# Backward weight products with 32x32 block transposes on VectorE in place of 128x128 transposes on TensorE

## The chip, the cores and the metric

The kernel runs on one core of a Trainium2 chip. A core has five engines with a queue each: TensorE (PE: matrix products and transposes into PSUM; its weight loads are shown as PEld), VectorE (DVE), ScalarE (ACT), GpSimd (POOL) and SyncE (SP, which here only issues loads). Sixteen DMA engines move data between HBM and the core's SBUF. The metric is the device time of one execution in microseconds. Lower is better.

## What is computed

A forward pass of four residual blocks for one new token of two sequences, and its whole backward pass. Blocks 1 and 3 are grouped-query attention over a long cache (32 query heads, 4 key/value heads, 16,384 positions, head size 128), blocks 2 and 4 an MLP (1024 to 3584 to 1024); both attention blocks share their weights, and so do both MLPs.

```python
def _A_ref(x, k_cache, v_cache, wq, wo):
    q = (x @ wq).reshape(B, Sq, Hq, Dh).transpose(0, 2, 1, 3)
    k, v = repeat(k_cache, rep), repeat(v_cache, rep)
    scores = einsum("bhqd,bhkd->bhqk", q, k) * (Dh ** -0.5)
    o = einsum("bhqk,bhkd->bhqd", softmax(scores), v)
    return o.transpose(0, 2, 1, 3).reshape(B, Sq, Hq * Dh) @ wo

def _B_ref(x, w1, b1, w2, b2):
    h = gelu(einsum("bsd,df->bsf", layernorm(x), w1) + b1)
    return einsum("bsf,fd->bsd", h, w2) + b2

x = A_x
x = x + _A_ref(layernorm(x), K, V, wq, wo)
x = x + _B_ref(layernorm(x), w1, b1, w2, b2)
x = x + _A_ref(layernorm(x), K, V, wq, wo)
x = x + _B_ref(layernorm(x), w1, b1, w2, b2)
out, grads = x, vjp(grad_out)   # gradients of x, K, V, wq, wo, w1, b1, w2, b2
```

In the backward pass every weight W [n_in, n_out] meets a gradient g of two columns: `W g`, a product over the columns of W. In memory W has its rows first, and a matrix product on PE sums over partitions. So W must be turned in some way before it can be multiplied. This case is about that turning.

## The kernel before

Everything is written out by hand in order (`manual_schedule`); each engine runs its queue in the order of the program, and a buffer's next load waits until the last reader of the buffer is done. Loads go into a pool `ld` of seven 1 MB buffers (`NLD = 7`, `LDW = 4096` columns of bf16 on 128 partitions). SP issues them in program order, so it runs ahead of the engines by up to seven buffers.

The stages in order, with their place in the profiled execution: attention forward of layer 0 (to about 172 us), passes over wo, w1 and w2 (to 257), q pass and attention forward of layer 1 (to 420), wo, w1 (to 448), then backward: w1 (453 to 474), wo (479 to 501), attention backward of layer 1 (502 to 660), then w2 (to 687), w1 (to 711) and wo (to 731) for layer 0, and the tail (from 732): attention backward of layer 0 with all outer products and the stores of the gradients.

*Weights as stationary operand.* A forward product needs no turning: `lhsT` is the weight block itself. `w_pass` (L288) does the forward product (L306), the backward product, or both on one load of W (w2 at L918, called w2a: forward of layer 0 and the product that layer 1's backward pass will need).

*Backward products.* `BwdPipe` (L260) takes a row of up to 1024 weights per partition: eight PE transposes into a PSUM bank (L270, tile `wtp`), one eviction to SBUF by ACT or DVE, whichever has been charged less (`evac_bf16`, L151; `charge`, `pick`), and two rows later eight products with the turned block as stationary operand and the gradient, repeated 16 times to 32 columns, as moving operand (L281).

*Ahead.* For the passes over w2 and wo of layer 0 (`w2b`, `wob`) the class `Ahead` (L343) turns rows in place before their gradient is there (`turn`, L318), so that PE and ACT turn rows while the layer norms in front run; `some(rest, n)` and the hooks of `ln_bwd` (L224) say how many. `copies_on("A")` (L139) sends those evictions to ACT. Products follow at L381. Every fifth row is not turned at all: `Dots` (L325) spreads the gradient along the free axis (L335), and DVE multiplies and sums the row, once per sequence (L339).

*wq in attention backward.* `attn_bwd` (L593) works in slots, one for each quarter of a V chunk. wq's four column quarters come in as their gradient gets ready (`wq_steps`, L877): the first two quarters and half of the third by dots (`by_dots`, L615), the rest by PE turns (L322, tile `wtq`) and products (L895).

*The tail.* Loads of K, V and wq come from a list of jobs (`load_next`, L1197; `pump`), evictions go to ACT or DVE by load, stores on POOL's queue. A quarter of wq is turned row by row (`late_pe`), and multiplied when its gradient is there. The last quarter's products (`in_rows`, L1281) are in front of the last layer norm.

*Loads of w1.* `w_chunks` (L245) gives one row block of 128 rows with all 3584 columns per load: 7,168 bytes in a row per partition. w2 and wo come as four row blocks of 1024 columns, 2,048 bytes in a row.

```python
tp = (pt if self.n % 3 else px)([128, 8, 128], BF16, "wtp")
for o in range(on):
    PE.transpose(tp[:, o, :], wv[:, j, (o0 + o) * 128:(o0 + o + 1) * 128], ident[:])
wT = ktp.tile([128, 8, 128], BF16, name="wT", tag="kT")
evac_bf16(wT[...], tp[...], on * 128)
...
PE.matmul(wide_out(self.out_ps, 2 * jj), lhsT=wT[:, o, :], rhs=wide_in(self.gT[:, o0 + o, :]), ...)
```

Of the kernel before, what the change touches and what calls it, by code (L numbers as in the profile page):

```python
# [23 lines left out]
def kernel(  # L24
# [24 lines left out]
    nc = tc.nc  # L49
# [72 lines left out]
    sel2v = sel2[:].rearrange("p (h t) -> p t h", t=2)  # L122
    e_all = pers.tile([128, G, NP, 2, 8, 2], BF16, name="e_all")
# [6 lines left out]
    V.memset(ACCT[:], 0.0)  # L130

# [128 lines left out]
    class BwdPipe:  # L260


        def __init__(self, out_ps, gT_bf, n_o):
            self.out_ps, self.gT, self.n_o, self.q, self.n = out_ps, gT_bf, n_o, deque(), 0

        def push(self, wv, j, jj, o0, on):
            self.n += 1
            tp = (pt if self.n % 3 else px)([128, 8, 128], BF16, "wtp")
            for o in range(on):
                PE.transpose(tp[:, o, :], wv[:, j, (o0 + o) * 128:(o0 + o + 1) * 128], ident[:])  # L270
            wT = ktp.tile([128, 8, 128], BF16, name="wT", tag="kT")
            evac_bf16(wT[:, 0:on, :].rearrange("p a b -> p (a b)"), tp[:, 0:on, :].rearrange("p a b -> p (a b)"),
                      on * 128)
            self.q.append((wT, jj, o0, on))
            if len(self.q) > 2:
                self.pop()

        def pop(self):
            wT, jj, o0, on = self.q.popleft()
            for o in range(on):  # L280
                PE.matmul(wide_out(self.out_ps, 2 * jj), lhsT=wT[:, o, :], rhs=wide_in(self.gT[:, o0 + o, :]),  # L281
                          start=(o0 + o == 0), stop=(o0 + o == self.n_o - 1))

        def flush(self):
            while self.q:
                self.pop()

    def w_pass(W, n_in, n_out, name, xT_bf=None, gT_bf=None, mid=None):  # L288

        JO, JI = n_out // 128, n_in // 128  # L290
        fps = bps = pipe = None
        if xT_bf is not None:
            nw = min(WIDE, 512 // JO)
            fps = ACCT[:, 0:JO * nw].rearrange("p (j b) -> p j b", b=nw)
            V.memset(fps, 0.0)
        if gT_bf is not None:
            bps = px([128, 512], F32, name + "_b")
            pipe = BwdPipe(bps, gT_bf, JO)
        for j0, rb in w_chunks(n_in, n_out):
            wv = w_load(W, j0, rb, n_out)  # L300
            if mid is not None and j0 == 4:
                mid()
            if fps is not None:
                for j in range(rb):
                    for jo in range(JO):
                        PE.matmul(fps[:, jo, :].rearrange("p (a b) -> p a b", b=2),  # L306
                                  lhsT=wv[:, j, jo * 128:(jo + 1) * 128],
                                  rhs=xT_bf[:, j0 + j, :].unsqueeze(1).to_broadcast([128, nw // 2, 2]),
                                  start=False, stop=True, skip_group_check=True)
            if bps is not None:  # L310
                for j in range(rb):
                    for o0 in range(0, JO, 8):
                        pipe.push(wv, j, j0 + j, o0, min(8, JO - o0))
        if pipe is not None:
            pipe.flush()
        return fps[:, :, 0:2] if fps is not None else None, pairs(bps, JI) if bps is not None else None
# [8 lines left out]
    class Dots:  # L325


        def __init__(self, name):
            self.rows = [ktp.tile([128, 2 * NB, 128], BF16, name=name, tag="blk", bufs=2) for _ in range(2)]
            self.junk = wrk.tile([128, D], BF16, name="junk", tag="rowout")  # L330

        def spread(self, b, col):
            tp = pt([128, 8, 128], BF16, "dotr")
            for o in range(8):
                PE.transpose(tp[:, o, :], col(o).to_broadcast([128, 128]), ident[:])  # L335
            evac_bf16(self.rows[b][:].rearrange("p a b -> p (a b)"), tp[:].rearrange("p a b -> p (a b)"), 1024)

        def dot(self, w, b, out):
            V.scalar_tensor_tensor(out=self.junk[:], in0=w, scalar=1.0, in1=self.rows[b][:].rearrange("p o d -> p (o d)"),  # L339
                                   op0=ALU.mult, op1=ALU.mult, accum_out=out)  # L340
            charge("D", 1.15)

    class Ahead:  # L343


        def __init__(self, W, n_in, name, xT_bf=None, fps=None):
            self.W, self.J, self.x, self.fps, self.name = W, n_in // 128, xT_bf, fps, name
            self.dotted = range(4, FJ, 5)
            self.dp = vec.tile([128, len(self.dotted), 2], F32, name=name + "_dp")
            self.chunks = list(w_chunks(n_in, D))  # L350
            self.rows = {}

        def load(self, k):
            j0, rb = self.chunks[k]
            wv = w_load(self.W, j0, rb, D)
            for j in range(rb):
                self.rows[j0 + j] = wv[:, j, :]

        def row(self, j):
            w = self.rows[j]  # L360
            if self.fps is not None:
                for jo in range(DJ):
                    PE.matmul(wide_out(self.fps, jo * WIDE), lhsT=w[:, jo * 128:(jo + 1) * 128],
                              rhs=wide_in(self.x[:, j, :]), start=False, stop=True, skip_group_check=True)
            if j not in self.dotted:
                turn(w, lambda: pt([128, 8, 128], BF16, "turn"))

        def spread(self, gT_bf):
            self.dd = Dots(self.name + "_g")
            for b in range(2):  # L370
                self.dd.spread(b, lambda o: gT_bf[:, o, b:b + 1])

        def dots(self, j):
            for b in range(2):
                self.dd.dot(self.rows[j], b, self.dp[:, self.dotted.index(j), b:b + 1])

        def products(self, j, out_ps, gT_bf):
            if j in self.dotted:
                return
            for o in range(8):  # L380
                PE.matmul(wide_out(out_ps, 2 * j), lhsT=self.rows[j][:, o * 128:(o + 1) * 128],  # L381
                          rhs=wide_in(gT_bf[:, o, :]), start=(o == 0), stop=(o == 7))
# [42 lines left out]
    class Acc:  # L425
# [3 lines left out]
        def __init__(self, g, src, coef, finish, half=0):  # L429
# [3 lines left out]
            self.acc = ACCT[:, half * 256:half * 256 + 256] if half < 2 else pm_([128, 256], F32, "acc2")[:]  # L433
# [158 lines left out]

    def attn_bwd(l, do_bf, dqT, dn, groups, ahead):  # L593
        sch = Sched()
        wq_q, wq_n, w2_q = deque(), {}, deque()
        slots = []
        for i, g in enumerate(groups):
            for c in range(NCH):
# [16 lines left out]
        def by_dots(kv):  # L615
# [7 lines left out]
            def item(j, b):  # L623
                if j % 4 == 0 and b == 0:
                    n[0][j // 4]()
# [918 lines left out]
```

## Time and profile before

| what | value |
|---|---|
| runs | 1138.20, 1139.32, 1139.52 us; median 1139.32 |
| span of the profiled execution | 1136.1 us |
| busy: PE | 945.3 us, 83% |
| busy: DVE | 637.6 us, 56% |
| busy: ACT | 567.5 us, 50% |
| mean granted TensorE clock | 0.882 |
| bytes moved | 449.24 MB, mean 395 GB/s |
| packets of the load queue q1 and the store queue q0, share of 16 engines | 77.4% and 19.7% |
| transposes of weights by `BwdPipe` (L270) | 928, 75.9 us |
| in-place turns of weights `wt` (L322) | 400, 31.1 us |
| dots of wq, w2, wo on DVE (L339) | 40, 10, 10; 48.8, 12.2, 12.3 us |
| in the chain that ended last | PE 50%, DMA 31%, DVE 10%, issue 4%, ACT 3% |

How to read it. The span is one execution under the profiler; the runs are timed without it. A busy share is an average over stages that have different limits: PE is busy 83% of the span, yet for most of it the DMA engines are what is full. The views by slice and by stage tell which it is where. In a line of groups, "x" is the number of instructions, then busy time and the mean duration of one; durations of instructions that follow each other overlap, so the time from start to start is shorter than the mean duration. Shares of DMA above 1 come from packets that overlap in the records. GB/s is the safer figure, but packets of 2 KB move at a lower rate than those of 8 KB even where the engines never stand.

### The profile page before, as it was taken

Reading aid. Unit: us, or ns where it says so; the run is one execution under the profiler, and the core shown is the slowest. Engines: PE = TensorE matmul, PEld = TensorE weight load, DVE = VectorE, ACT = ScalarE, POOL = GpSimd, SP = SyncE. Lnnn points to the kernel's source line nnn. Section 1 sums busy time; section 2 is a strip of 40 time slices with the busy share of each in tenths; the row PEclk is TensorE's granted clock in tenths of the full one; section 3 lists DMA queues with packets and bytes.
Section 4 is the critical chain, followed back from the end, with each engine's and each line's share of the span. In section 5 each row is a group of like instructions: output and inputs, shape, how many; then the busy total and the mean of one; then the engine's idle time right before and its main releaser. Section 6 shows DMA issues by size and latency. Waiting matters only on the chain.

```text
span 1136.1 us, 38923 instructions
## 1 busy us (share of the span) xinstructions
PE 945.3 (83%) x17087; PEld 715.0 (63%) x17087; DVE 637.6 (56%) x1391; ACT 567.5 (50%) x1414; POOL 70.1 (6%) x124
## 2 busy tenths in 40 slices
PE   4978796487879885899998699988898897898896
PEld 3867675487767665898876588855555454455452
DVE  1545442133545432444746454778788767787776
ACT  0544342022535340344554344767787756686674
POOL 0000000000000000000000000022111111111210
PEclk9988976596998976899998899999999978898987
DMA  9999999998999989999999999998999999999997
GB/s 371 424 424 424 424 425 412 405 379 354 423 426 424 423 320 422 392 350 393 380 422 418 359 371 336 364 367 311 394 418 423 423 419 423 424 412 421 422 402 288
DMA packets 91962, 449.24 MB, mean 395 GB/s; under 512 B 7302, under 2 KB 7302, under 8 KB 54672
## 3 DMA queue, kind: packets, MB, share of 16 engines
q1 hardware_dynamic: 74448, 354.46, 77.4%
q0 software_dynamic: 17344, 92.29, 19.7%
q8 instruction: 133, 2.18, 0.7%
q14 instruction: 37, 0.30, 0.1%
HBM read 348.14 MB, written 98.58 MB: 393 GB/s over the span
## 4 chain that ended last, share of the span: by engine, by line
PE 50%; DMA 31%; DVE 10%; issue 4%; ACT 3%; POOL 0%; DVEq 0%; POOLq 0%; ACTq 0%; SPq 0%
DMA kv_V<-in_A_v_cache_dram 13%; PE tp L420 10%; PE wtp L270 5%; DMA kv_K<-in_A_k_cache_dram 5%; PE tpm L1451 4%; PE acc_all L452 4%; PE xm L1260 4%; DMA wt<-in_A_wo_dram 3%; DMA out_dram<-keepK 3%; DMA keepK<-in_A_v_cache_dram 3%; PE sc L573 3%; PE turn L322 3%; PE xm L1174 3%; PE dp L1313 2%; DMA out_dram<-keepxV 2%
## 5 line engine op out<-in xcount | busy, mean ns | idle before, releaser
L153 ACT COPY kT<-tp 128x512 int32<-128x512 int32 x209 | 122.8, 587 | 256.7 <-PE tp L420 247.9
L156 DVE COPY kT<-tp 128x1024 bf16<-128x1024 bf16 x159 | 108.8, 691 | 110.0 <-PE tp L420 99.1
L420 PE MATMUL tp<-ident,kv_K 128*128 128x128 bf16 x1728 | 140.3, 228 | 4.5 <-DMA kv_K<-in_A_k_cache_dram 4.5
L420 PEld LDWEIGHTS <-kv_K 128*128 128x128 bf16 x1728 | 106.3, 102 | 5.4 <-DMA kv_K<-in_A_k_cache_dram 5.3
L164 DVE CAST big<-xm 128x512 bf16<-128x512 f32 x133 | 86.4, 685 | 16.2 <-PE xm L1260 11.2
L161 ACT CAST big<-xm 128x512 bf16<-128x512 f32 x151 | 82.2, 595 | 23.2 <-PE xm L1260 13.0
L573 PEld LDWEIGHTS <-kT 128*128 128x128 bf16 x2048 | 75.9, 98 | 27.3 <-issue 21.0
L573 PE MATMUL sc<-qT_bf,kT 128*128 128x8 bf16 x2048 | 91.7, 171 | 0.3 <-issue 0.3
L161 ACT CAST keepV<-xm 128x512 bf16<-128x512 f32 (+1 forms) x137 | 75.1, 594 | 28.5 <-PE xm L1260 16.6
L420 PE MATMUL tp<-ident,kv_V 128*128 128x128 bf16 x864 | 71.5, 231 | 11.5 <-DMA kv_V<-in_A_v_cache_dram 10.6
L270 PE MATMUL wtp<-ident,wt 128*128 128x128 bf16 x928 | 75.9, 229 | 4.3 <-issue 2.9
L537 ACT ACTIVATE e_all<-sc,negm 128x64 bf16<-128x64 f32 x256 | 77.2, 345 | 1.1 <-DVE negm L532 1.0
L164 DVE CAST keepV<-xm 128x512 bf16<-128x512 f32 (+1 forms) x101 | 66.1, 685 | 18.6 <-PE xm L1260 12.3
L306 PEld LDWEIGHTS <-wt 128*128 128x128 bf16 x1696 | 48.8, 103 | 42.9 <-issue 15.2
L452 PE MATMUL acc_all<-kv_V,e_all 128*16 128x256 bf16 x864 | 46.2, 294 | 29.7 <-DMA kv_V<-in_A_v_cache_dram 16.7
L156 DVE COPY wT<-wtp 128x1024 bf16<-128x1024 bf16 (+1 forms) x64 | 41.1, 645 | 47.7 <-PE wtp L270 43.9
L153 ACT COPY wT<-wtp 128x512 int32<-128x512 int32 (+1 forms) x60 | 34.1, 568 | 64.2 <-PE wtp L270 55.8
L420 PEld LDWEIGHTS <-kv_V 128*128 128x128 bf16 x864 | 56.7, 103 | 13.3 <-DMA kv_V<-in_A_v_cache_dram 11.3
L270 PEld LDWEIGHTS <-wt 128*128 128x128 bf16 x928 | 58.1, 102 | 5.0 <-issue 3.7
L537 ACT ACTIVATION_READ_ACCUMULATOR e_all<-sc,negm 128x1 f32 x256 | 60.1, 235 | 0.0
L161 ACT CAST keepK<-xm 128x512 bf16<-128x512 f32 x98 | 52.9, 596 | 13.5 <-PE xm L1260 7.6
L1313 PE MATMUL dp<-wdo,kT 128*128 128x64 bf16 x896 | 52.2, 205 | 0.0
(369 smaller groups left out, 1750.5 us busy)
## 6 DMA issues: line engine op xcount, KB each, us to landing
kv_K<-in_A_k_cache_dram SPq DMA_DIRECT2D x81, 1024.0 KB, 11.5
kv_V<-in_A_v_cache_dram SPq DMA_DIRECT2D x81, 1024.0 KB, 12.5
wt<-in_A_wo_dram SPq DMA_DIRECT2D x32, 1024.0 KB, 9.9
wt<-in_B_w_dram SPq DMA_DIRECT2D x32, 896.0 KB, 14.0
out_dram<-big POOLq DMA_DIRECT2D x26, 1024.0 KB, 19.0
out_dram<-keepV POOLq DMA_DIRECT2D x19, 1024.0 KB, 20.0
out_dram<-keepK POOLq DMA_DIRECT2D x17, 1024.0 KB, 17.8
wt<-in_A_wq_dram SPq DMA_DIRECT2D x16, 1024.0 KB, 9.0
```

Source lines behind the costliest of these rows:

```text
L153: S.copy(out=dst.bitcast(I32), in_=src.bitcast(I32))
L156: V.tensor_copy(out=dst, in_=src)
L161: S.copy(out=dst, in_=src)
L164: V.tensor_copy(out=dst, in_=src)
L270: PE.transpose(tp[:, o, :], wv[:, j, (o0 + o) * 128:(o0 + o + 1) * 128], ident[:])
L306: PE.matmul(fps[:, jo, :].rearrange("p (a b) -> p a b", b=2), lhsT=wv[:, j, jo * 128:(jo + 1) * 128], rhs=xT_bf[:, j0 + j, :].unsqueeze(1) ...
L420: PE.transpose(tp[:, j, :], cv[:, b * 8 + j, :], ident[:])
L452: PE.matmul(self.acc[cg:cg + 16, :], lhsT=coef(u), rhs=self.cv[:, t:t + 2, :].rearrange("p t d -> p (t d)"), start=False, stop=True, tile_ ...
L537: S.activation(out=e_all[:, g, f * half:(f + 1) * half, l, h, :], in_=sc[g][f][:, h, :].rearrange("p (a b) -> p a b", b=2), func=ACT.Exp, ...
L573: PE.matmul(sc[g][f][:, :, t % TH], lhsT=kT[:, j, :], rhs=q_bf[:, g, :], start=True, stop=True)
L1260: PE.matmul(pss[k][:], lhsT=blk[p:p + 64, o + 2 * h + k // 2, :], rhs=Qm[p:p + 64, :, :].rearrange("p a b -> p (a b)"), start=True, stop=T ...
L1313: PE.matmul(dp[:, :, t:t + 4], lhsT=kT[:, j, :], rhs=wd[:, :, x:x + 4], start=(b + j == 0), stop=False)
```

## The change

No backward weight product is transposed by PE any more, and the dots go too. The idea of the new form: take a weight tile [128 rows, columns] and see each pair of neighbouring bf16 columns as one 4-byte word. DVE transposes the words in 32x32 blocks, in place (`turn32`). Partition 32q + c of a block then holds the pairs of column pair c, and along the free axis run the 32 rows of the group q. So partitions now index columns, as a product needs, but the four groups of 32 partitions hold different rows. The gradient therefore becomes a block-diagonal stationary operand of eight columns (four row groups q by two sequences, `spread_g`): for each group of partitions only its own two columns are non-zero. One product takes 32 of the original columns; a tile of 1024 columns takes 32 products, spread over four column groups of PE, with all four row blocks of a tile as 128 moving columns at a step of two elements (`products`). They add up in a PSUM bank that has been set to zero (`Wide`). At the end of a pass `columns` transposes the bank to SBUF by DVE in 32x32 blocks, and four f32 matmuls with the constant `fold` add the column groups and set the result into columns.

What is added per pass: a memset of each bank, 16 small matmuls and one DVE multiplication for the gradient (per 1024 columns), and the column step. What is moved:

- w1 is read in column strips of 1024 columns by four row blocks, and a last one of 512 columns by eight (`w_tiles`), in its forward passes too.
- w2a: the turns of a tile stand behind the forward product of the next tile; the last tile's turns and the column step go between the tiles of the following q pass (`between`).
- wq in attention backward: a quarter's two loads 1 and 5 slots after its gradient is ready, turns from 8 slots later on, products 16 slots later; the last quarter's loads 1 and 3 slots after the last group's start. All quarters add into one half of a bank, and one column step at the end gives the gradient.
- w2b and wob: `some(rest, n)` now turns four rows of w2b and nine of wob on DVE around the layer norms; the eighth load of wob follows the first tile's products.
- the tail: turns of wq rows on DVE; each quarter has its own memset or first write, products and column step.

```diff
+    strip = const.tile([128, 4], F32, name="strip")
+    V.tensor_reduce(out=strip[:], in_=identf[:].rearrange("p (q c) -> p q c", c=32), axis=AX.X, op=ALU.add)
+    fold = const.tile([128, 32], F32, name="fold")
+    V.tensor_reduce(out=fold[:], in_=identf[:].rearrange("p (q c) -> p c q", c=32), axis=AX.X, op=ALU.add)
...
+    def turn32(view):
+        w = view.bitcast(I32)
+        V.transpose(out=w, in_=w)
+        charge("D", 0.06 + w.shape[-1] / 960.0)
+    def spread_g(gT, o0, on, G8, bank):
+        ps = bank[:, 0:on * 8].rearrange("p (o k b) -> p o k b", k=4, b=2)
+        for k in range(4):
+            at = k // 2 * 64 + k % 2
+            for q in range(4):
+                PE.matmul(ps[32 * q:32 * q + 32, :, k, :], lhsT=ident[:, at:at + 63:2], rhs=gT[:, o0:o0 + on, :],
+                          start=True, stop=True, tile_position=(0, 32 * q))
+        n = on * 4
+        V.tensor_tensor(out=G8[:, o0 * 4:o0 * 4 + n], in0=bank[:, 0:n * 2]..., in1=strip[:]..., op=ALU.mult)
+    def products(wv, G8, n0, acc, fresh=False):
+        for n in range(wv.shape[2] // 32):
+            cg = 32 * (n % 4)
+            at = n // 2 * 64 + n % 2
+            PE.matmul(acc[cg:cg + 8, :].rearrange("p (j r) -> p j r", r=32),
+                      lhsT=G8[:, n0 + n].rearrange("p q b -> p (q b)"), rhs=wv[:, :, at:at + 63:2],
+                      start=fresh and n < 4, stop=True, tile_position=(0, cg), skip_group_check=True)
+    def columns(acc, fin):
...
+        V.transpose(out=x, in_=acc)
+        xv = x.rearrange("p (n m) -> p n m", m=32)
+        for q in range(4):
+            PE.matmul(fin[32 * q:32 * q + 32], lhsT=fold[:], rhs=xv[:, :, 2 * q:2 * q + 2], start=True, stop=True,
+                      tile_position=(0, 32 * q))
+    def w_tiles(W, n_in, n_out):
+        if n_out == 1024:
...

+        elif n_out < 4096:
+            for c0 in range(0, n_out, 1024):
+                cw = min(1024, n_out - c0)
+                nj = 4096 // cw
+                for j0 in range(0, n_in // 128, nj):
+                    out.append((j0, nj, c0, cw))
...
+    def w_bwd(W, n_in, n_out, gT, fin, name, mid=None):
...
+        for k, (j0, nj, c0, cw) in enumerate(w_tiles(W, n_in, n_out)):
+            wv = w_take(W, j0, nj, c0, cw)
+            if j0 == 0:
+                spread_g(gT, c0 // 128, cw // 128, Gw, pm_([128, 512], F32, "spg"))
+            for j in range(nj * cw // 1024):
+                turn32(wv.rearrange("p j n -> p (j n)")[:, j * 1024:(j + 1) * 1024])
+            q.append((wv, j0, nj, c0))
+            if len(q) > 1:
+                pop()
...
+        def wq_now(kv):
+            n = wq_job(kv)
             n[1]()
-            for b in range(2):
-                wq_q.append(lambda b=b: dd.spread(b, lambda o: dq_all[:, kv * 8 + o, 2 * l + b:2 * l + b + 1]))
...
+            for k, at in ((0, 1), (1, 5)):
+                sch.later(at, n[0][k])
+                for j in range(4):
+                    sch.later(at + 8 + 2 * j, n[2][4 * k + j])
+                sch.later(at + 16, n[3][k])
...
-    g2 = attn_in_bwd(1, g3, dn1, lambda: some(rest, 2), lambda: some(rest, 3))
+    some(rest, 2)
+    g2 = attn_in_bwd(1, g3, dn1, lambda: some(rest, 1), lambda: some(rest, 1))
...
+    w2b.open(gM_all[:, 0:DJ, lsl(0)])
+    for k in range(len(w2b.tiles)):
+        some(rest, 4 if k else 0)
+        w2b.tile(k)
...
-    dn = ln_bwd(dm[:], sv["y2"][:], sv["rstd2"][:], "dn", lambda: some(rest, 2), lambda: some(rest, 3))
-    dx = ln_bwd(dn[:], sv["y1"][:], sv["rstd1"][:], "dx", lambda: some(rest, 1), lambda: some(rest, 4))
+    some(rest, 4)
+    dn = ln_bwd(dm[:], sv["y2"][:], sv["rstd2"][:], "dn", lambda: some(rest, 1), lambda: some(rest, 1))
+    some(rest, 1)
+    dx = ln_bwd(dn[:], sv["y1"][:], sv["rstd1"][:], "dx", lambda: some(rest, 1), lambda: some(rest, 1))
...
+    def quarter_end(ps):
+        fin = ps[:, 256:256 + 2 * DJ].rearrange("p (j b) -> p j b", b=2)
+        columns(ps[:, 0:256], fin)
+        V.tensor_tensor(out=dn0[:], in0=dn0[:], in1=fin, op=ALU.add)
```

## The prediction

> **What bounds the kernel now.** I read the slices of the span first, then busy time by stage, then the groups and the chain of waits inside the weight stages. The slices (page, part 2; 28.4 us each):
>
> ```profile
> DMA  9999999998999989999999999998999999999997
> GB/s 371 424 424 424 424 425 412 405 379 354 423 426 424 423 320 422 392 350 393 380 422 418 359 371 336 364 367 311 394 418 423 423 419 423 424 412 421 422 402 288
> ```
>
> Over most of the span the DMA engines are full (424 GB/s): only bytes count there. The dips are the stages that read weights for backward products, and the opening of the tail. Busy time by stage (us; busy and count for PE, PEld, DVE, ACT, POOL; then clock, DMA share, GB/s):
>
> ```profile
> 248.00:264.00 16.00, 11.04 (x311) 10.52 (x309) 4.99 (x16) 3.05 (x6) 0.69 (x1) 0.86 0.68 245
> 264.00:416.00 152.00, 131.05 (x2747) 109.74 (x2748) 71.63 (x157) 69.28 (x302) 0.00 (x0) 0.90 1.01 421
> 428.00:453.30 25.30, 13.10 (x319) 11.94 (x315) 7.26 (x36) 0.25 (x1) 2.11 (x5) 0.61 1.02 425
> 478.90:502.40 23.50, 21.95 (x503) 21.66 (x502) 11.04 (x20) 9.50 (x17) 0.00 (x0) 0.94 0.96 360
> 548.00:560.00 12.00, 11.92 (x271) 9.28 (x269) 9.58 (x18) 6.59 (x12) 0.00 (x0) 1.00 0.87 326
> 636.00:660.00 24.00, 16.48 (x307) 13.11 (x308) 9.41 (x24) 10.26 (x20) 0.00 (x0) 0.93 0.87 321
> 660.00:687.40 27.40, 25.45 (x677) 24.90 (x677) 15.61 (x42) 14.56 (x25) 0.00 (x0) 0.94 0.98 368
> 687.40:710.70 23.30, 20.99 (x473) 19.77 (x471) 13.18 (x37) 9.70 (x18) 0.71 (x1) 1.00 0.96 346
> 710.70:731.60 20.90, 20.20 (x452) 19.08 (x448) 15.58 (x40) 16.71 (x29) 0.00 (x0) 1.00 0.94 348
> ```
>
> From 660 to 732 PE is busy 90 to 97% and DMA falls behind: a serial chain (layer norm, pass over w2, over w1, two layer norms, pass over wo) sets the time, and what it gains or loses reaches the tail whole. The same holds from 453 to 528. Inside a pass the chain of waits shows the price of one row (1024 weights per partition), eight transposes and eight products, 0.46 + 0.19 = 0.65 us, with the eviction alternating on ACT and DVE beside it:
>
> ```profile
> 458.37 0.46 PE wtp L270 x8
> 458.82 0.19 PE dm_ps_b L281 x8
> ```
>
> **The new price of a row.** One VectorE transpose of 128x512 4-byte words in place ("turn" below); no row shows one. Nearest rows: four f32 casts of 128x512 in a train, and as low bound the 128x512 f32 memset of L295, 0.48 us. In the built order 240 of them stand on DVE's queue: 28 for w2a, 28 and 32 for the two passes behind it, 32 for wq, and the same again (w2b, w1, wob, wq).
>
> ```profile
> 763.28 2.48 DVE L164 CAST keepV<-xm 128x512 bf16<-128x512 f32 x4 [1.28 <-PE xm L1260]
> 737.90 0.98 PE acc_all L452 x32
> 643.42 7.70 DMA wqt<-in_A_wq_dram
> ```
>
> 2.48/4 = 0.62 with the last one's tail, 0.605 from start to start. I take 0.605; the ends are 0.48 (memset) and 0.685 (the cast's full duration). The kernel's own load accounting charges it 0.593, and its charge for the ACT copy, 0.597, meets a measured 0.587. The Trainium skill (VectorE: DVE Perf Modes, The three transpose paths) gives 311 ns for 128x128 bf16, which no row here shows; as an estimate from that page, 384 more cycles at 0.96 GHz make 711 ns, and by it the sum below would be some 16 us worse.
>
> So a row goes from 0.65 us of PE (with two engines evicting beside it) to 0.605 us of DVE: hardly a gain where the row rate sets the time. Products: 8 per row as before, but 128 columns wide with an 8-column weight load, in four column groups. L452 (256 wide, four groups) runs 32 in 0.98 us, 31 ns each; I take 35 ns, 1.1 us a tile of four rows, hidden behind its 2.4 us of turns. Bounds: 25 ns (0.80 us for the 32 of L306) and 100 ns (no overlap of groups, strided operand).
>
> **Where it lands, stage by stage.**
>
> A, before 264. w1 is now read in column strips: per row 3 packets of 2 KB and one of 1 KB in place of one of 7 KB. The packet records have medians of 84 ns (2,048 B), 159 (4,096), 272 (7,168), 309 (8,192), a line of 9 ns + 0.0366 ns per byte; 1 KB is then 46.5, and a row 298.5 against 272. 1,024 rows x 26.5 ns / 16 engines = 1.7 us a pass (0 to 4.1 if 1 KB took as long as 2 KB), four passes. The first forward pass ends 1.7 later. Then w2a: PE now takes 3.4 us a tile (0.80 forward, 4 x 0.65); after, DVE's 2.42 sets it. 6 tiles x 2.42 from 231 end at 245.9 against 256.5, and the seventh tile's turns move into the q pass. Buffers come free ahead of wq's loads. DMA's standstill of 248 to 264, 16 x (1 - 245/421) = 6.7 us, shrinks to about 2.2, since the seventh wq load needs the buffer of the postponed tile; behind it on SP's queue stand the last wq load and K's first ones. A = 1.7 - 4.5 = -2.8; what follows is DMA-bound, so it is kept.
>
> B, 428 to 530. w1 forward +1.7 (DMA-bound: share 1.02). w1 backward, 20.8 us from dh to dm: memset 0.27, spreading the gradient 0.8 (16 matmuls at the 45 ns of L573), multiply 0.45 (as L642's 256 wide, 0.42), 28 turns 16.9, three more multiplies 1.3, last products 0.7, the column step (a 256-wide transpose of PSUM 0.4, as the f32 copy acc_sb; four f32 matmuls 0.6, as L467; copy 0.2) 1.2 = 21.7: +0.9. wo backward, 22.2 from 478.9: two memsets 1.0, multiply 0.45, 32 turns 19.4, products 1.1, column step 1.4 = 23.4: +1.2. The turns wait behind the layer norm's small operations on DVE's queue; PE used to start transposing during them. The strips of this pass cost DMA another 1.7, and those of the pass in D too; I count them at nothing, since the row rate sets both passes (turns 16.9, strips 298.5 x 64 ns = 19.1 with the loads two to three tiles ahead); without that lead they cost 1.7 each. B = +3.8.
>
> C, attention backward. The 40 dots (1.22 us each on DVE) go; a quarter's 8 turns take 4.8 us of DVE in place of 16 x 1.27 = 20. The dots held their weight buffers until 650, and SP's last loads behind them; PE stood 7.7 us for a quarter's weights (last line above). Standing: 12 x (1 - 326/421) = 2.7 and 24 x (1 - 321/421) = 5.7. SP now issues a quarter's two loads one and five slots after its gradient (the last one's one and three), ahead of the K and V loads of the next slots, and the turns follow eight slots on, so the loads delay K and V by nothing that seven buffers don't cover. I take 2.3 and 2.7 of the standing back (the rest is the end of the chain): C = -5.0; none to all gives 0 to -8.4.
>
> D, 660 to 731.6, DVE's queue item by item. Gradient of the last quarter to dn: 2.2 before; casts 0.3, spread 0.8, multiply 0.45, 64 products 2.2, column step 1.4 = 5.2: +3.0. Layer norm: three turns that no wait covers, +1.8. w2b, 21.5 before: memsets 0.9, multiply 0.45, 24 turns 14.5, products 1.1, column steps and multiply 1.6 = 18.6: -2.9. w1, 23.2: copies that stood beside PE 1.0, memset 0.3, multiplies 1.8, 28 turns 16.9, the output row and block work that shares DVE 3.4, end 1.9 = 25.3: +2.1. Two layer norms, 4.4: four turns ahead of them 2.4, three uncovered 1.8 = 8.6: +4.2 (PE and ACT did ten rows in their shadow). wob, 16.4: 1.4 + 23 turns 13.9 + 1.1 + 1.4 = 17.9: +1.5. D = +9.7. The tail's opening keeps PE, DVE and ACT busy alike, so it moves as a whole; its own turns replace evictions of equal length.
>
> E, the ends: column step in front of the last layer norm, +1.2. The two new constants of the opening are two reductions of some 0.2 us under the first loads, nothing.
>
> Sum: -2.8 + 3.8 - 5.0 + 9.7 + 1.2 = +6.9 us. The profiled span of 1136.1 becomes 1143.0; runs have a median of 1139.32, 3.2 above the span, so 1146.
>
> The clock: where PE is thin it is granted less (0.61 from 428 to 453, PE busy 13.1 of 25.3) and a layer norm's pair of f32 matmuls takes 0.60 us (474.79) against 0.34 (711.38). Weight passes will be about as thin; I have not added this. The Trainium skill (TensorE: Matmul & The Clock Gate, Part 1) says the clock is released only by sustained activity. By the row alone the sum stays; by the rule some eight such pairs and column steps cost 0.3 each, 2 to 3 us more.
>
> **Rivals.** (1) Faster: the turn is cheap. Break-even is 6.9 us over the 148 rows of B and D, 0.047 each, a turn of 0.558. At the memset's 0.48: 148 x 0.125 = -18.5, so 1128. For it: 4-byte in-place data in SBUF, no PSUM; against: the train of casts. (2) Nothing to see: gains and losses cancel, turn near 0.56 or C taken whole; 1137 to 1141.6. (3) PE becomes the bound: column groups don't overlap on a strided operand, 100 ns a product, 3.2 us a tile against 2.42; 37 tiles x 0.8 = +30, 1176. Against it: L452 at 31 ns with the same groups. (4) Turns at the cast's full 0.685: +11.8, 1158; it is the upper part of my own case.
>
> **Numbers.** My case (with 4) has 0.58, rival 1 0.23, rival 2 0.10, rival 3 0.09. 0.2% (2.3 us) is about what a measurement here can tell from none. Slower 0.58 + 0.09 = 0.67, same 0.10, faster 0.23. My case alone runs 1142 to 1158; for 8 in 10 the range takes in most of rival 1 and leaves out rival 3: 1130 to 1161.
>
> **What would show it.** StreamTranspose of 128x512 near 0.6 us from start to start; no standstill of DMA between 248 and 256; PE waiting for DVE from the old 455 on; attention backward without its 7.7 us wait; from dq's last scaling to the tail's first dof about 81 us against 71.6; products at 25 to 40 ns. I am wrong if the turn is under 0.56, if DMA can't fill the new strips at that packet line, or if the tail's opening absorbs the delay.

## The result and the profile after

The changed kernel takes 1169.87 us (median of four runs) against 1139.42: a ratio of 1.0278, 95% interval 1.0246 to 1.031. The forecast was 1146 with a range of 1130 to 1161. The direction was right; the loss is 30 us where 7 were forecast. Of all executions in this document one, of e11, took 1358.91 us against 1138 to 1142 for its fellows; it is not counted. The profiled execution has a span of 1167.2 us against 1136.1, a difference of 31.1. The slices of the new page (part 2; 29.2 us each):

```profile
PEclk9988895559888955589996655589997968797978
DMA  8999999999999989999998697797999999999996
GB/s 372 423 424 424 425 424 411 395 419 423 406 424 425 394 307 402 351 374 401 396 415 347 219 357 259 283 359 279 383 416 421 419 420 423 423 418 420 424 406 278
```

The dip of 379 and 354 GB/s behind the first pass over w2 is gone (419, 423). New are two holes: 347 and 219 at the end of attention backward (slices 22 and 23), and 259 and 283 in the passes behind it (slices 25 and 26). In slices 22 to 26 the PE clock is at 0.5 to 0.6. The 279 of slice 28 lies in the tail already; slice 28 of the kernel before has 311. By stage (us; busy and count for PE, PEld, DVE, ACT, POOL; then clock, DMA share, GB/s), the stages cut as in the table of the kernel before:

```profile
237.50:253.50 16.00, 10.41 (x304) 9.12 (x308) 12.25 (x29) 0.00 (x0) 0.69 (x1) 0.50 1.03 423
426.10:451.40 25.30, 10.70 (x291) 9.99 (x292) 7.04 (x34) 0.25 (x1) 2.10 (x5) 0.55 1.05 403
476.60:500.80 24.20, 9.41 (x291) 7.78 (x291) 22.39 (x42) 0.00 (x0) 0.00 (x0) 0.50 0.90 344
548.00:560.00 12.00, 11.14 (x254) 8.74 (x251) 5.81 (x11) 6.43 (x12) 0.00 (x0) 1.00 0.84 315
626.00:648.00 22.00, 8.37 (x113) 5.84 (x113) 4.84 (x9) 2.66 (x5) 0.00 (x0) 0.50 0.67 258
648.00:672.00 24.00, 15.36 (x295) 12.11 (x291) 7.84 (x18) 4.91 (x10) 0.00 (x0) 0.71 0.69 236
681.50:708.80 27.30, 13.70 (x448) 11.88 (x448) 17.47 (x31) 0.00 (x0) 0.00 (x0) 0.50 0.89 308
708.80:733.20 24.40, 11.39 (x300) 8.21 (x299) 21.45 (x53) 1.33 (x3) 0.71 (x1) 0.50 0.82 279
733.20:758.90 25.70, 9.36 (x292) 7.84 (x292) 24.48 (x58) 0.00 (x0) 0.00 (x0) 0.57 0.73 270
```

In the passes over w1 and wo (third row and the last two) DVE is busy 88 to 95%, as forecast: it sets them. In the pass over w2b (681.5 to 708.8) it is busy 64% only, and from 626 to 672 neither an engine nor DMA is full (PE 38 and 64%, DMA share 0.67 and 0.69). Those two stretches hold the surprise.

The span cut at values that both traces have (us from one to the next, read from DVE's timeline; "forecast" is what the prediction's terms make of the difference):

| from ... to | before | after | difference | forecast |
|---|---|---|---|---|
| start ... dh_all of layer 1 (A and w1 forward) | 453.1 | 451.4 | -1.7 | -1.1 |
| ... its dof (w1 and wo backward) | 48.0 | 48.1 | +0.1 | +2.1 |
| ... last scaling of dq (attention backward) | 158.8 | 171.7 | **+12.9** | -5.0 |
| ... cast of g2 (dn, layer norm) | 6.2 | 10.2 | +4.0 | +4.8 |
| ... dh_all of layer 0 (w2b) | 21.4 | 27.3 | **+5.9** | -2.9 |
| ... dm_sb (w1) | 23.2 | 24.4 | +1.2 | +2.1 |
| ... cast of g1 (two layer norms) | 4.4 | 8.1 | +3.7 | +4.2 |
| ... the tail's first dof (wob) | 16.5 | 17.6 | +1.1 | +1.5 |
| ... end | 404.5 | 408.3 | +3.8 | +1.2 |

Seven of nine rows are within 3 us of the forecast. Attention backward is off by 17.9 us and w2b by 8.8, together 26.7; the whole sum was short by 24.2.

### The profile page after: what moved, and what is told of

Same layout as the page of the kernel before. It is cut to its first block, busy times and chain, and to the rows that moved or that the text cites. A ratio compares the mean times of both kernels' runs of the same rounds, so it can differ in the third digit from the quotient of the medians.

```text
span 1167.2 us, 36523 instructions
## 1 busy us (share of the span) xinstructions
PE 889.1 (76%) x15974; PEld 635.2 (54%) x15975; DVE 652.5 (56%) x1421; ACT 501.7 (43%) x1301; POOL 70.1 (6%) x124
## 2 busy tenths in 40 slices
DMA packets 104176, 449.09 MB, mean 385 GB/s; under 512 B 7238, under 2 KB 11334, under 8 KB 66896
## 5 line engine op out<-in xcount | busy, mean ns | idle before, releaser
L162 DVE COPY kT<-tp 128x1024 bf16<-128x1024 bf16 x147 | 100.4, 690 | 120.8 <-PE tp L469 111.9
L469 PE MATMUL tp<-ident,kv_K 128*128 128x128 bf16 x1728 | 147.1, 235 | 4.8 <-DMA kv_K<-in_A_k_cache_dram 4.8
L269 DVE STREAM_TRANSPOSE wt<-wt 128x512 int32<-128x512 int32 x176 | 107.2, 673 | 9.0 <-PE w2b_f L354 9.0
L167 ACT CAST big<-xm 128x512 bf16<-128x512 f32 x180 | 96.9, 596 | 31.9 <-PE xm L1299 24.1
L354 PEld LDWEIGHTS <-wt 128*128 128x128 bf16 x1920 | 56.5, 105 | 50.6 <-issue 18.2
L170 DVE CAST keepV<-xm 128x512 bf16<-128x512 f32 (+1 forms) x102 | 66.5, 682 | 19.7 <-PE xm L1299 12.7
L170 DVE CAST big<-xm 128x512 bf16<-128x512 f32 x104 | 67.5, 679 | 9.8 <-PE xm L1299 6.9
L170 DVE CAST keepK<-xm 128x512 bf16<-128x512 f32 x82 | 52.5, 678 | 9.2 <-PE xm L1299 4.8
L679 DVE TENSOR_TENSOR dX<-dp,e_all 128x256 bf16<-128x256 f32 x32 | 13.5, 422 | 77.1 <-PE dp L673 77.1
L296 PEld LDWEIGHTS <-blocks 128*8 128x8 bf16 x1472 | 32.5, 107 | 43.5 <-issue 36.3
L1299 PE MATMUL xm<-QmK,blk 64*128 64x512 bf16 x256 | 50.3, 457 | 2.4 <-ACT keepV L167 1.0
```

The source lines that it names most:

```text
L162: V.tensor_copy(out=dst, in_=src)
L167: S.copy(out=dst, in_=src)
L170: V.tensor_copy(out=dst, in_=src)
L269: V.transpose(out=w, in_=w)
L354: PE.matmul(fps[:, o0 + o, :].rearrange("p (a b) -> p a b", b=2), lhsT=wv[:, j, o * 128:(o + 1) * 128], rhs=x[:, j0 + j, :].unsqueeze(1).t ...
L469: PE.transpose(tp[:, j, :], cv[:, b * 8 + j, :], ident[:])
```

## Experiments

The kernel before had medians of 1138.9 to 1141.2 us beside these runs. "Attention backward", "w2b" and so on are the rows of the table above. Each row comes from the one profiled execution of a run; e1, e2, e3, e5, e8 and e9 have two executions each, which differ by up to 6.6 us. The rows say more than the run's time there: attention backward took 171.7, 172.3 and 171.7 us in the changed kernel, e1 and e9, whose code for it is the same.

**e1: w2b's products one tile later.** In the pass over w2b each row has a forward product that must read the weights before DVE turns them in place. DVE's timeline of the changed kernel there (start, us, line, operation, and in brackets the idle time before it and who ended it):

```profile
684.38 2.49 DVE L269 STREAM_TRANSPOSE wt<-wt 128x512 int32<-128x512 int32 x4 [1.45 <-PE w2b_f L354]
688.31 2.49 DVE L269 STREAM_TRANSPOSE wt<-wt 128x512 int32<-128x512 int32 x4 [1.44 <-PE w2b_f L354]
692.25 2.49 DVE L269 STREAM_TRANSPOSE wt<-wt 128x512 int32<-128x512 int32 x4 [1.44 <-PE w2b_f L354]
```

A tile takes 3.93 us of which 2.49 are turns; for 1.44 DVE waits for the forward product `w2b_f`. In PE's order that product stands behind the products of the tile before, and these wait for that tile's last turn: a ring over two engines.

```diff
     for k in range(len(w2b.tiles)):
-        some(rest, 4 if k else 0)
+        some(rest, 4)
         w2b.tile(k)
```

> One edit: in the pass over w2b the products of a tile stand on PE behind the forward rows of the next tile, not ahead of them. Theory (order): the turns wait 1.44 us in each of six tiles for the forward rows of their own tile, which PE holds behind the products of the tile before. With the edit the tile period falls from 3.93 us to about 2.5, from g2's cast to dh_all 27.3 falls to about 18.5 to 20, the run from 1169.9 to about 1161 to 1163. Rival (late loads): the period is set by w2b's or w1's loads; then it stays at 3.5 us or more, or the gain is lost again in the pass over w1, and the run stays within 2 us of 1169.9.

Measured: 1160.33 us; w2b 19.1 us in place of 27.3, all other rows within 1 us. DVE's timeline of e1:

```profile
683.40 13.90 DVE L269 STREAM_TRANSPOSE wt<-wt 128x512 int32<-128x512 int32 x23
698.22 0.71 DVE L269 STREAM_TRANSPOSE wt<-wt 128x512 int32<-128x512 int32 x1 [0.92 <-PE w2b_f L354]
```

23 turns follow each other at 0.604 us and none of them waits for a load. The order of PE's queue explains the 8.2 us.

**e2, e3, e5: the load buffers in attention backward.** SP's queue of the changed kernel at the end of attention backward, then two rows of PE, then what PE waited for from 600 to 672 (total, times, longest):

```profile
607.31 0.38 SPq L920 DMA_DIRECT2D wqt<-in_A_wq_dram  x1
...
611.49 1.17 SPq L920 DMA_DIRECT2D wqt<-in_A_wq_dram  x2
...
624.87 0.38 SPq L920 DMA_DIRECT2D wqt<-in_A_wq_dram  x1
626.03 7.31 SPq L458 DMA_DIRECT2D kv_K<-in_A_k_cache_dram  x2
641.57 0.33 SPq L458 DMA_DIRECT2D kv_V<-in_A_v_cache_dram  x1
648.17 0.33 SPq L458 DMA_DIRECT2D kv_K<-in_A_k_cache_dram  x1
651.27 0.33 SPq L458 DMA_DIRECT2D kv_V<-in_A_v_cache_dram  x1
```

```profile
659.59 1.02 PE L296 MATMUL acc<-wqt,blocks 128*8 128x128 bf16 x32
...
664.67 0.65 PE L296 MATMUL acc<-wqt,blocks 128*8 128x128 bf16 x32
```

```profile
PE tp L469 <- DMA kv_V<-in_A_v_cache_dram: 14.2, 6, 4.8
PE acc_all L501 <- DMA kv_K<-in_A_k_cache_dram: 12.0, 5, 4.3
```

Four wq tiles are asked for between 607 and 625; the first two are released by their products at 659.6 and 664.7, the other two (the last quarter's) after 672. From 625 to 659 K and V go through three of the seven buffers, and after 626 SP issues a load only every 3 to 10 us. From 600 to 672 PE waits 26 us for K and V. Three edits, each alone:

```diff
e2, the last quarter's loads and turns:
-                    for k, at in ((0, 1), (1, 3)):
+                    for k, at in ((0, 12), (1, 13)):
                         sch.later(at, n[0][k])
                         for j in range(4):
-                            sch.later(at + 6 + j + 2 * k, n[2][4 * k + j])
+                            sch.later(18, n[2][4 * k + j])
e3, the first three quarters:
-                    sch.later(at + 8 + 2 * j, n[2][4 * k + j])
-                sch.later(at + 16, n[3][k])
+                    sch.later(at + 8 + j, n[2][4 * k + j])
+                sch.later(at + 12, n[3][k])
e5, the last quarter's tiles in two other buffers:
-            wt = ld.tile([128, LDW], BF16, name="wqt", tag="ld") if get_ is None else get_("wq", kv, j)
+            wt = own[j] if own else ld.tile(...) if get_ is None else get_("wq", kv, j)
...
+    n = wq_n["last"] = wq_job(g % HKV, {0: held_tiles["K"], 4: held_tiles["V"]})
```

> One edit: in attention backward the last quarter's two wq loads are issued 12 and 13 slots after the last group's start in place of 1 and 3, behind its last V load, and its eight turns together in slot 18. Theory (buffers): from 612 to 672 four of the seven load buffers hold wq tiles, K and V stream through three, DMA stands. With the edit two are held at most; of the 12.9 us that attention backward lost (dof to the last scaling 158.8 to 171.7) 9 to 14 come back: run 1156 to 1161. Rival (DVE's turns among the slots delay the evictions and dX): turns are as many as before, so no more than 2 us come back. Rival (PE's clock of 0.5 from 630 is the cause and not the effect): 0.5 stays from 630 to 660 and at most 3 us come back.

> One edit: the turns of the first three quarters of wq in attention backward follow each other slot by slot in place of every second slot, and the products come 12 slots after the load in place of 16. Theory (buffers): seven tiles at 2.49 us are a ring of 17.4 us, a wq tile held 20 us stops SP's queue once per tile; shorter by 5 us, the SP waits on the products of wq (12.1 us in three waits) go down to under 5 and the standing at 550 to 560 (295 GB/s) shrinks; the four held buffers at the end stay. Run 1163 to 1167. Rival (only the last quarter's early loads matter): within 2 us of 1169.9. Rival (turns every slot crowd DVE): slower by 2 us or more.

> The last quarter's two wq tiles of layer 1 lie in two buffers outside the ring of seven (those that keep the first K and V chunk of one group for the tail, so that this chunk's part of the outputs is computed from other data); the order and the slots of all loads, turns and products stay. Theory (buffers): the standstill of 633 to 668 goes, dof to the last scaling falls from 171.7 by 9 to 15 us, run 1155 to 1161. Rivals (order of SP's queue, DVE's turns, the clock by itself): all of these are as before, so within 2 us of 1169.9.

Measured: e2 1157.36 us, attention backward 159.0; e3 1165.87, 167.9; e5 1155.97, 156.4 (171.7 in the changed kernel). From 626 to 648 in e2, and in e5:

```profile
626.00:648.00 22.00, 16.40 (x253) 12.84 (x254) 7.12 (x14) 5.99 (x11) 0.00 (x0) 0.64 0.87 340
```

```profile
626.00:648.00 22.00, 14.11 (x212) 11.31 (x214) 9.04 (x18) 5.14 (x10) 0.00 (x0) 0.61 0.99 391
```

DMA moves 340 and 391 GB/s where the changed kernel moved 258. e5 is a probe of time alone: its two other buffers are those that keep one chunk of K and V for the tail, so part of its outputs comes from other data. It decides: order of the loads, slots of the turns and work of DVE are as in the changed kernel, and two more buffers alone bring 15.3 us of that row. So neither the turns between the slots nor the low clock by itself held attention backward up. e3 gained the time that was expected (4.0 us), but not in the way that was expected: SP's waits on the products of wq stayed at 12.2 us in all (12.1 before; under 5 expected). Each got shorter (longest 5.9 in place of 9.0), and three became six. From 550 to 560 DMA moved 302 GB/s against 295, hardly more. Where e3's 4 us come from is open.

**e9: no turns ahead of the layer norms.** The five turns that stand on DVE ahead of the two layer norms in front of wob are left to the pass behind them (two `some(rest, ...)` lines taken out).

> One edit: the five turns of wob that stand on DVE ahead of the two layer norms (four and one) come behind them; the four inside the layer norms stay. Theory (DVE's queue from dm_sb to dof is what counts, wherever the turns stand): dm_sb to gA's cast 8.1 to about 5.1, gA's cast to dof 17.6 to about 20.6, the tail's first dof within 0.8 us of 758.9, run within 2 us of 1169.9. Rival (the later turns hide behind loads that are late anyway): the pass stays at 17.6 to 19, run 2 to 3 us less.

DVE's timeline of e9:

```profile
734.02 0.17 DVE L1104 COPY dm_sb<-dm_fin 128x16 f32<-128x16 f32 x1 [0.43 <-PE dm_fin L308]
...
739.45 0.17 DVE L1110 CAST gA_all<-gM 128x16 bf16<-128x16 f32 x1
...
740.99 16.72 DVE L269 STREAM_TRANSPOSE wt<-wt 128x512 int32<-128x512 int32 x28
...
760.00 0.19 DVE L885 TENSOR_TENSOR dof<-wob_fin,rbc 128x32 f32<-128x32 f32 x1
```

The layer norms take 5.4 us in place of 8.1, the pass 20.5 in place of 17.6, the sum 26.0 against 25.7; the run 1169.32. So it doesn't matter where the turns stand: what counts is that 32 of them at 0.6 us, and little beside them, go through one engine.

**e4 and e7: the edits together, and PE's rows back.** e4 is e1, e2 and e3 in one. e7 adds that PE and ACT turn the first tile of w2b and the first two of wob in the shadow of the layer norms, as the kernel before did, with ordinary products that go straight into columns:

```diff
+            if j < 4 * self.np:
+                turn(w.rearrange("p j n -> p (j n)"), lambda: pt([128, 8, 128], BF16, "turn"))
+            else:
                 turn32(w.rearrange("p j n -> p (j n)"))
...
+            if k < self.np:
+                for j in range(4):
+                    for o in range(8):
+                        PE.matmul(self.fin[:, 4 * k + j, :], lhsT=self.wv[k][:, j, o * 128:(o + 1) * 128],
+                                  rhs=self.gT[:, o, :], start=(o == 0), stop=(o == 7))
+                return
```

> The three edits together (w2b's products one tile later, the last quarter's wq loads at slots 12 and 13, the first three quarters' turns in each slot and products at 12). Theory (two separate causes, held load buffers and the order in w2b's pass): the gains add up: dof to the last scaling 171.7 to 154 to 157, g2's cast to dh_all 27.3 to 19.1, so the tail's first dof from 758.9 to about 734; of that the tail keeps most and gives some back (it grew by 5 us where it began 14 to 17 us earlier): run 1144 to 1150. Rival (one cause behind both, PE's clock of 0.5): they overlap, run above 1153.

> The three edits, and in the shadow of the layer norms PE and ACT turn rows again as in the kernel before: the first tile of w2b and the first two of wob by 128x128 transposes with ordinary products, no turn of DVE ahead of the layer norms, 12 turns fewer on DVE. Theory (D's loss at the layer norms is DVE's queue): dm_sb to gA's cast 8.1 to 4.5 to 5.5, last scaling to g2's cast 10.2 to 8 to 9, gA's cast to dof 17.6 to 13 to 16; the tail's first dof 5 to 9 us before that of the three edits alone, run 1138 to 1143, level with the kernel before. Rival (DMA sets the pass over wo): the pass takes back what the layer norms gain, run within 2 us of the three edits.

e4: 1145.8 us, ratio to the kernel before 1.0058 (1.0035 to 1.0081); attention backward 155.5, w2b 18.9, first dof of the tail at 732.8. The separate gains in time (12.5 + 4.0 + 9.5 = 26.0) become 24.1 together. By the rows they hardly overlap: attention backward gives 16.1 where e2 and e3 gave 12.7 and 3.8, w2b 8.4 where e1 gave 8.2. That fits two separate causes and not one behind both. e7: 1140.88, ratio 1.0018 (0.9998 to 1.0037), as expected in time. Its rows fell short: the two layer norms 5.9 (4.5 to 5.5 expected), wob 17.0 (13 to 16), and the end of dq to g2 grew to 11.1 (8 to 9), of which DVE waits 3.1 us for `w2b_f` ahead of the one turn that was left there. First dof is at 729.2, 3.6 us before e4's (5 to 9 expected) and 2.4 before the old kernel's. The profiled execution ends level with the old one, but it was the fastest of ten (1138.05).

**e8 and e11: w1 by rows.** The forward passes over w1 read rows of 7 KB again, in the changed kernel (e8) and in e7 (e11).

```diff
-        wv = wt[:].rearrange("p (j n) -> p j n", j=nj)
+        wv = wt[:, 0:nj * cw].rearrange("p (j n) -> p j n", j=nj)
...
-        for j0, nj, c0, cw in w_tiles(W, n_in, n_out):
+        for j0, nj, c0, cw in ([(j, 1, 0, n_out) for j in range(n_in // 128)] if n_out == F
+                               else w_tiles(W, n_in, n_out)):
```

> One edit: the two forward passes over w1 read whole rows again (7 KB packets, 896 KB a tile); the backward passes keep the strips. Theory (packet line): 1.7 us less in each forward pass, first h_all 228.9 to 227.2, dh_all of layer 1 3.4 us earlier or less where the waits of DMA cover it; run 1166 to 1169. Rival (strips cost nothing beside the queue): first h_all within 0.4 us of 228.9, run within 1.5 us of 1169.9.

> The version with the three edits and PE rows at the layer norms, w1 read by whole rows in the forward passes. Theory (packet line, and the tail passes gains on): the tail's first dof 2 to 4 us earlier than 729.2, run 1138 to 1140. Rival (the tail's stores and loads take the gain back, as in the run with rows alone, where first dof came 4.1 us earlier and the end 0.6): run within 1 us of 1140.9.

e8: first h_all at 227.9 in place of 228.9 (1.0 us; 1.7 expected), dh_all of layer 1 2.4 us earlier, the tail's first dof 4.1 earlier, the end 0.6; run 1171.63 from two executions, which settles nothing at this size. e11: 1140.92, ratio 1.0017 (1.0005 to 1.003), no better than e7; its first dof comes at 728.0, 1.2 us earlier than e7's where 2 to 4 were expected. The strips cost 1.0 us of the 1.7 that the packet line gave in the first forward pass, and 2.4 of 3.4 in the two. That the tail took this back is what the two traces look like, but a single execution varies by as much: it is not shown.

**e10: PE kept busy.** Each turn of the passes is followed on PE by 6 (w2b: 3) transposes of the constant `ident` that nobody reads, on top of e7.

> The version with the three edits and PE rows at the layer norms, and with each DVE turn of the backward passes of layer 1 (w1, wo) and of the last ones (w2b, w1, wo) PE gets 6 (w2b: 3) transposes of a constant whose result nobody reads, so that it is busy in those passes. Theory (the thin PE's clock of 0.5 costs time of its own): the clock from 451 to 513 and from 677 to 750 goes to 0.9 or more, the layer norms' pairs, the last products and the tail's opening are shorter, the tail's first dof 2 to 4 us and the end 3 to 6 us earlier: run 1135 to 1138. Rival (the slow clock is only a mark of waiting, what waits is set by DVE and DMA): clock up, run within 1.5 us of 1140.9 or longer by what the idle transposes hold up.

The stages of e10 over w1 and the two layer norms behind it:

```profile
690.00:713.50 23.50, 18.86 (x478) 16.71 (x470) 21.41 (x52) 1.23 (x3) 0.71 (x1) 0.91 0.89 305
713.50:718.00 4.50, 4.15 (x62) 3.71 (x61) 3.98 (x20) 3.40 (x7) 0.00 (x0) 1.00 1.04 394
```

Against e7 the clock rose from 0.50 to 0.91 in the pass and from 0.64 to 1.00 in the layer norms, and these fell from 5.9 to 4.5 us. The end of dq to g2, w1 and wob got shorter too, by 0.5, 1.0 and 0.5. But w2b rose from 17.4 to 20.2, attention backward, which the edit doesn't touch, from 155.1 to 159.3 (not explained), and the run takes 1145.02: 4 us more than e7. The idle transposes take PE's time themselves, so the run doesn't price the clock cleanly. What it shows is some 3.3 us in the four rows that got shorter, of a loss of 30.

**e13: the last quarter of wq by PE,** its 64 products straight into columns, on top of e7.

> The version with the three edits and PE rows at the layer norms, and the last quarter of wq in attention backward is turned by PE and evicted by ACT or DVE as in the kernel before, its 64 products go straight into columns, without spreading and column step behind the last gradient (the other three quarters' column step runs beside the products). Theory (spread, multiply and column step are the 2 to 3 us more between the last scaling and dn): last scaling to g2's cast 11.1 to 8 to 9, run 1137 to 1140. Rival (PE's slow clock makes 64 products of 128x128 weights as long as the spread, products and column step): 11 as before, run within 1 us of 1140.9.

Last scaling to cast of g2 9.7 in place of 11.1, but w2b 20.8 in place of 17.4 and attention backward 156.6 in place of 155.1: 1146.22 us. Its aim was met in part and more was lost beside it; why w2b grew stays open.

**e14: part A alone.** The kernel before, with only w2a's products in the new form (its forward rows as they were, w1 by rows):

```diff
+    def w2a_turn(k, lo=0, hi=4):
+        for j in range(lo, hi):
+            turn32(a_wv[k][:, j, :])
+        if hi == 4:
+            products(a_wv[k], a_G, 0, a_acc.at(4 * k, 4))
...
+        if k:
+            w2a_turn(k - 1)
...
+    x3 = attn_layer_fwd(1, x2_, deque([lambda: w2a_turn(NW2 - 1, 0, 2), lambda: w2a_turn(NW2 - 1, 2, 4), w2a_end]))
```

> The kernel before with one part of the change alone: the backward products of the first pass over w2 (w2a) by DVE turns, block-diagonal gradient and column step, the last tile in the following q pass; w1's loads by whole rows and every other pass as before. Theory (DMA's standstill behind w2a, 6.7 us in the kernel before, shrinks by 4 to 5 and what follows is bound by DMA, so it is kept): from the first h_all to the next n_all 33.1 to about 21, dh_all of layer 1 at 448.5 to 449.5 (453.1 before), everything behind it 4 us earlier up to the tail, of which the tail keeps all or gives back up to 3: run 1135 to 1138.5. Rival (attention forward gives it all back): dh_all within 1 us of 453.1, run within 1 us of the kernel before.

Measured: 1132.81 us against 1139.42, ratio 0.9941 (0.9922 to 0.996): faster than both kernels, and better than the 1135 to 1138.5 expected. Behind w2a the stage in which DMA moved 245 GB/s in the kernel before:

```profile
248.00:264.00 16.00, 9.22 (x304) 8.46 (x303) 4.89 (x12) 0.00 (x0) 0.60 (x1) 0.50 1.01 423
```

The standstill of 6.7 us is gone entirely; dh_all of layer 1 comes at 448.0 in place of 453.1, and the profiled span is 1131.0, 5.1 shorter: the tail keeps all of it.

## Why the prediction was right and wrong, step by step

**The turn: right.** DVE's timeline of the changed kernel in the pass over w1:

```profile
452.37 4.86 DVE L269 STREAM_TRANSPOSE wt<-wt 128x512 int32<-128x512 int32 x8
457.15 0.39 DVE L281 TENSOR_TENSOR Gw<-spg,strip 128x256 bf16<-128x256 f32 x1
457.45 4.85 DVE L269 STREAM_TRANSPOSE wt<-wt 128x512 int32<-128x512 int32 x8
```

Eight in 4.86 us with the tail of the last one (0.67 is the mean duration of one): 0.60 from start to start. That is the price that the prediction took from the casts (0.605). The 711 ns worked out in the prediction from the Trainium skill (VectorE: DVE Perf Modes, The three transpose paths) is not met; the measurement decides. With it falls rival 1, which needed 0.558 or less, and rival 4.

**The products: right.** 32 take 0.65 us at full clock and 1.02 at half (the two rows of PE above): 20 and 32 ns each, about the 25 to 40 that were named. Rival 3 with 100 ns is out.

**A: right in sign, the gain somewhat larger.** I let 2.2 us of DMA's standstill stay for the postponed tile's buffer; nothing stayed (423 GB/s from 237.5 to 253.5, and the same in e14), so w2a alone is worth 5.1 us in e14 where 4.5 were forecast. The strips took some of it back, 1.0 us in the first forward pass where 1.7 were forecast. Over all four passes the packets rose from 91962 to 104176 and the time of the hardware queue's packets from 77.4% of 1136.1 to 76.0% of 1167.2 us, 879 to 887: 8 us by shares rounded to 0.1, where 4 x 1.7 = 6.8 were worked out. The packet line itself held: a packet of 1 KB took 46 ns in the median, where it gave 46.5.

**B: slightly too dear.** w1 backward 20.5 us (21.7 forecast), wo 22.9 from cast to dof (23.4): +0.1 in sum against +2.1, with the strips hidden behind turns as assumed.

**C: wrong, and the larger of the two errors.** The step that failed is "the loads delay K and V by nothing that seven buffers don't cover". I counted how early the loads are issued and not how long a tile stays. The ring of seven comes round in 7 x 2.49 = 17.4 us at full DMA (1 MB at 421 GB/s). A quarter's tile was planned to stay 16 slots from load to products, and near the end, where two quarters overlap, four of seven stayed 48 to 60 us (the first from 607.31 to 659.59, the last from 624.87 to past 672). In place of the -5.0 came +12.9; e5, e2 and e3 give 15.3, 12.7 and 3.8 us of it back, and with e2 and e3 together (e4) attention backward is at 155.5, 3.2 under the kernel before. So 3.2 of the 5.0 that C promised were there, behind a loss that the schedule made.

**D: right but for w2b.** The end of dq to g2, w1, the layer norms and wob are each within 1 us. For w2b "24 turns 14.5, products 1.1" put the products beside the next tile's turns, as in the passes over w1 and wo. Here the forward product of the next tile stands between, in place of free turns; I had not followed PE's order. Six waits of 1.44 are 8.6 us; with the order mended the pass takes 18.9 (e4) to 19.1 (e1), where 18.6 were forecast.

**E: too small.** The tail took 3.8 us more, not 1.2. In its first ten us DMA moved 277 GB/s against 357 before, and the clock was 0.78 against 1.00 (the first row is the changed kernel, the second the kernel before):

```profile
758.90:768.90 10.00, 9.55 (x178) 7.10 (x178) 4.20 (x17) 3.71 (x7) 1.11 (x2) 0.78 0.73 277
```

```profile
731.60:741.60 10.00, 9.17 (x198) 6.38 (x198) 5.74 (x21) 4.48 (x9) 1.11 (x2) 1.00 0.93 357
```

Every version with the new tail needs 407 to 414 us for it, e14 with the old one 404.3 (404.5 before), so the loss may lie in the tail's own part of the change, in the loads that reach it late or in the clock; which of them, no run separates.

**The clock, which the prediction left out of its sum:** 2 to 3 us were named there from the Trainium skill (TensorE: Matmul & The Clock Gate, Part 1). The trace shows 0.50 without a break from 436 to 503 and from 672 to 746, with PE busy 41 and 45%:

```profile
436.00:503.00 67.00, 27.32 (x819) 23.81 (x819) 50.23 (x122) 1.06 (x3) 0.77 (x4) 0.50 1.00 383
672.00:746.00 74.00, 33.09 (x970) 27.22 (x971) 57.49 (x143) 1.33 (x3) 0.71 (x1) 0.50 0.81 281
```

In e10, with PE busy 80% in the pass over w1, it is 0.91 there. That agrees with the page, and the 3.3 us of e10's shorter rows are near the 2 to 3 named; it wasn't what decided.

## What to carry to other kernels

When a load is moved, hold the time for which its buffer stays taken, from issue to last use, against the time in which the ring of buffers comes round: held longer, a tile stands in the way of the loads behind it, however early it was issued itself. Here four of seven held 48 to 60 us against 17.4 cost 12 to 15 us; where the cost begins was not measured, and e3, with a shorter hold, left SP's waits as long in sum. When work moves to another engine, follow the order of both engines through one round of the loop; an operation in place must wait for whoever reads the old content, and work that stands ahead of that reader can close a ring. Try a change that is made in eight places in one of them as well: here the one place where DMA stood still because PE was full gives 0.6% alone, and the others hid it.

## What the runs showed of the hardware

VectorE turns 128x512 4-byte words in place in 0.60 us from start to start (eight in 4.86 us), as long as a 128x512 f32 cast from PSUM (four in 2.48 us). Four column groups with an operand at a step of two elements gave one 128-column product per 20 ns at full clock (32 in 0.65 us) and per 32 ns at half (32 in 1.02 us). PE's granted clock stayed at 0.50 for 74 us at a stretch where PE was busy 45% of the time, and a filler of transposes that took PE to 80% raised it to 0.91 without making the kernel faster. The kernel before itself spreads over 1134.8 to 1146.5 us in 17 runs, which is more than several of the differences looked for here.
